# Attention's sums of squares on ScalarE head by head, and four other steps of a fused attention and expert kernel at new places

## The chip, the cores and the metric

The kernel runs on one core of a Trainium2 chip. A core has a matrix engine (TensorE, PE in the profile, its weight loads PEld), a vector engine (VectorE, DVE), an activation engine (ScalarE, ACT), a general engine (GpSimd, POOL) and a queue that issues transfers (SyncE, SP). Each engine takes its instructions in the order in which the program lists them, and waits on semaphores for the others. The metric is the time of one launch on the device in microseconds, the median of several runs; lower is better.

## The reference, cut to what matters

```python
# attention, without softmax: batch 4, 8 heads, 576 tokens, 64 wide
kv = einsum('bhsd,bhse->bhde', k, v)
out = einsum('bhsd,bhde->bhse', q, kv)
rms = sqrt(mean(out * out, axis=-1, keepdims=True) + 1e-06)     # one per token and head
x = (out / rms * g_norm)                                        # 2304 tokens x 512
# first expert layer: x 2304 x 512, w_in 512 x 2048, w_out 2048 x 512
h = x @ w_in
x = (h * (1.0 / (1.0 + exp(-h)))) @ w_out
# second: 4 experts, w1 512 x 1024 and w2 1024 x 512 each, p = normed domain_probs
for e in range(4):
    out += p[:, e:e+1] * (maximum(x @ w1[e], 0.0) @ w2[e])
```

Everything is float32.

## The kernel before, in words

The kernel has three stages that overlap at their seams. All products are made in two or three parts: an operand is split into a high part (a rounded copy, made on ScalarE) and a low part (the difference, made on VectorE or GpSimd), and PE multiplies the parts.

*Attention* (the first 130 us). PROGRAM is a list of steps written out by hand order, one word each, that the kernel walks through; it fixes the order on every engine. For each of the four batches: `kv` multiplies keys and values, `bd` copies the result, `out` (attn_out, L702 to L716) makes the attention output of a block of 128 tokens in PSUM, `sq` (attn_sq, L718) its sums of squares per head, `cp` (attn_cp, L724) copies the block from PSUM to SBUF, `rms` (attn_rms, L727) makes 1/rms of all blocks of the batch, `sc` scales, `x` transposes (L763) and `xs` splits. The blocks number 4, 5, 4 and 5 for batches 0 to 3, 18 in all. In batch 0 the blocks have PSUM banks of their own, and rms uses a square root on ScalarE (L734); in the others the output tiles share four PSUM buffers with the first layer's products, `cp` frees them, and rms is made by multiplications on VectorE or GpSimd. The steps `cv1` (two activations, L634 and L635), `cv2` and `cv3` turn weights from a 64-bit form into float32; `sp` splits weights (L664, L665). The words `1:n`, `e:n`, `f:n` and `2:n` are steps of the first expert layer: its first product (mm1, L789), the evaluation of h (L803, L804), its split (L812, L813) and its second product (mm2, L827). In before, attn_sq squares the whole block on ScalarE (one activation of 128x512) and adds each head's 64 squares on VectorE (L722).

*First expert layer* (to about 475 us). Units of 12 matmuls of 128x512 each, PE busy throughout.

*Second expert layer* (class Second, the rest). It is made by Winograd's form of Strassen's scheme: seven products instead of eight, on sums and differences of the quarters. It runs in 24 steps: three passes over thirds of the tokens, eight half experts ("pairs" in what follows, numbered 0 to 7) each. Steps 0 to 7, the first pass, make the weights: sums of quarters (sumw, L202) and splits (op1, op2, L159 and L160); the split weights of the first layer of experts and of the second are put away to memory (put_away, L218) and got back (get, L223) in the later passes. In each step `first` (L251) makes seven products into two PSUM tiles x and z; the results c11, c12, c22 and c21 are collected (keep, add), rectified and multiplied with the probabilities (relu, L286), and split (oph). c21 is rectified straight from PSUM. In the first pass `second` (L332) makes the plain eight products for the second layer; from step 8 on `again` makes seven (L251 too, into ps_ox and ps_oz), for which t1 to t4 are differences of the c (sumh, L292), and `gather` (L310) adds results up.

The weight sums s1 to s4 of the second layer aren't used in the first pass, so they are made beside other work, all on VectorE but for the high part: for pair n, s1 and s2 in step 2n and s3 and s4 in step 2n + 1, until step 15.

The order on all engines in this stage comes from `events` (L372): each action is put at a slot, a number on a common scale on which PE has about one product to a slot, and the actions are then sorted and issued in that order. A step is 15 slots long in the first pass and 14 later. A slot is no time: it only says behind and ahead of what an instruction stands in its engine's queue. At the end of step 23 the results are transposed and written (leave_last, L364 to L369).

Of the kernel before, what the change touches and what calls it, by code (L numbers as in the profile page):

```python
# [13 lines left out]
AF = mybir.ActivationFunctionType  # L14
ALU = mybir.AluOpType
AX = mybir.AxisListType
PSUM = bass.MemoryType.PSUM

B, H, S, D = 4, 8, 576, 64
# [61 lines left out]
class Second:  # L81
# [290 lines left out]
    def events(self):  # L372
# [3 lines left out]
        def put(slot, f, *a):  # L376
            ev.append((slot, len(ev), f, a))

        pool = self.nc.gpsimd
        for n in range(self.steps):  # L380
            t, q = divmod(n, E2)
            b0, after = self.start[n], self.start[n + 1]
# [19 lines left out]
            for k in range(7):  # L402
                i = b0 + 1 + 2 * k
# [28 lines left out]
            put(b0 + 10.3, self.relu, n, "c22")  # L432
            put(b0 + 10.5, self.oph, n, "c22", None if make and n else pool)
            put(b0 + 12.25, self.relu, n, "c12")
            put(b0 + 14.05, self.relu, n, "c21")
            put(b0 + 14.06, self.ps.pop, (n, "x"))
            if make:
                put(b0 + 12.5, self.oph, n, "c12")
                put(b0 + 14.1, self.oph, n, "c21")
                for i, name in ((5.4 if n else 6.2, "c11"), (12.6, "c22"), (12.6, "c12"), (14.2, "c21")):  # L440
                    put(b0 + i, self.f.pop, (n, name))

                for k, (i, j) in enumerate(((0, 0), (0, 1), (1, 0), (1, 1))):
                    at = b0 + ((7.2, 8.6, 10.2, 14.7) if n else (7.2, 8.6, 15.2, 17.7))[k]
                    put(at - 5.5, self.load2, n, i, j)
                    put(at, self.op2, n, f"a{i + 1}{j + 1}", pool if k != 1 else None)
                    put(at + 0.01, self.raw.pop, (n, 2, f"a{i + 1}{j + 1}"))
                    if k != 2:
                        put(at + 2.5, self.put_away, n, 2, (0, 1, None, 6)[k])
                for b in range(4):  # L450
                    for d in range(2):
                        put(after + 4 * b + 2 * d, self.second, n, b, d)
                    put(after + 4 * b + 3.2, self.gather, n, b, *self.BLOCKS[b])
                    put(after + 4 * b + 3.21, self.ps.pop, (n, b))
                for i in range(2):
                    for j in range(2):
                        put(after + (10.1, 14.1)[1 - j], self.h.pop, (n, f"b{i + 1}{j + 1}"))
                        put(after + (6.1, 14.1)[i], self.w2.pop, (n, f"a{i + 1}{j + 1}"))
            else:
                put(b0 + 12.3, self.sumh, n, "t1")  # L460
                put(b0 + 12.31, self.f.pop, (n, "c12"))
                put(b0 + 12.4, self.oph, n, "t1")
                put(b0 + 12.5, self.sumh, n, "t2")
                put(b0 + 12.51, self.f.pop, (n, "c22"))
                put(b0 + 12.52, self.f.pop, (n, "t1"))
                put(after + 1.11, self.oph, n, "t2")
                put(after + 1.12, self.sumh, n, "t3")
                put(after + 1.13, self.f.pop, (n, "c11"))
                put(after + 1.14, self.oph, n, "t3", pool)
                put(after + 1.15, self.f.pop, (n, "t3"))  # L470

                u = after + (1 if n < self.steps - 1 else 3)
                put(u + 0.16, self.sumh, n, "t4")
                put(u + 0.17, self.f.pop, (n, "t2"))
                put(after + 5.5, self.oph, n, "t4", pool)
                put(after + 5.51, self.f.pop, (n, "t4"))
                put(after + 3.3, self.oph, n, "c21")
                put(after + 3.31, self.f.pop, (n, "c21"))
                for m, k in enumerate(self.ORDER):
                    put(after + 2 * m, self.again, n, k)  # L480
                    put(after + 2 * m - self.LEAD, self.get, n, 2, k)
                for m, g in enumerate(self.GATHER):
                    last = n == self.steps - 1
                    if last and m == 6:
                        for d in range(2):
                            put(after + 2 * m + 0.45, self.gather, n, *g, d)
                    else:
                        put(after + 2 * m + (1.1 if m < 6 else 0.45), self.gather, n, *g)
                put(after + 11.2, self.ps.pop, (n, "oz"))
                put(after + 12.46, self.ps.pop, (n, "ox"))  # L490
# [10 lines left out]
            elif q == E2 - 1:  # L501
                for k in range(PW // 256):
                    put(self.start[n + 3 + k] + 11.5, self.leave, n + 2 + k, t, 2 * k)

        for n in range(E2):
            a, b = self.start[2 * n] + (7 if n == 0 else 0), self.start[2 * n + 1] + (3 if n == 0 else 0)
            for k, (i, j) in enumerate(((1, 0), (1, 1), (0, 0), (0, 1))):
                put(a + 0.4 + 0.1 * k, self.load2, n, i, j, True)
            for at, name in ((a, "s1"), (a + 2, "s2"), (b, "s3"), (b + 2, "s4")):
                k = self.A.index(name)  # L510
                put(at + 5.5, self.sumw, n, 3, name)
                put(at + 7.3, self.op2, n, name)
                put(at + 9.2, self.put_away, n, 2, k)
                put(at + 9.21, self.w2.pop, (n, name))
            for name, at in (("s1", a + 7.6), ("a22", a + 5.6), ("a11", b + 5.6), ("a21", b + 5.6), ("s3", b + 7.4),
                             ("a12", b + 7.6), ("s2", b + 7.6), ("s4", b + 9.4)):
                put(at, self.raw.pop, (n, 3, name))
# [14 lines left out]
def attention_moe_kernel(ctx: ExitStack, tc: tile.TileContext, kv, qt, g2, probs, wd, w, out):  # L532
    nc = tc.nc
# [166 lines left out]
    rinv, ssq, o_ps, x_ps = {}, {}, {}, {}  # L700
# [17 lines left out]
    def attn_sq(b, i):  # L718
        p = o_ps[i]
        sq = tmp_p.tile([128, H, D], F32, tag="tmp", name="sq")  # L720
        nc.scalar.activation(sq.rearrange("p h d -> p (h d)"), p, AF.Square)
        nc.vector.reduce_sum(ssq[b][:, i, :], sq, axis=AX.X)  # L722

    def attn_cp(b, i):  # L724
        nc.scalar.activation(o_of[i].rearrange("p h d -> p (h d)"), o_ps.pop(i), AF.Copy)  # L725
# [117 lines left out]
    def order(e):  # L843
        return ([0, 1, 2, 3, 4], [4, 0, 1, 2, 3], [4, 0, 1, 2, 3], [0, 1, 4, 2, 3])[e]
# [5 lines left out]
    def put(i, h, f, *a):  # L850

        todo.setdefault((i, h), []).append((f, a))
# [5 lines left out]
    with tc.manual_schedule():  # L858
# [3 lines left out]
        for t in kvbd:  # L862
# [3 lines left out]

        do = dict(
            lkv=load_kv, lq=load_q, lwd=load_wd, kv=attn_kv, bd=attn_bd, out=attn_out, sq=attn_sq, cp=attn_cp,
            rms=attn_rms, sc=attn_scale, x=attn_x, xs=attn_xs, cv1=cv1, cv2=cv2, cv3=cv3, sp=split,
        )  # L870
# [27 lines left out]
        for e in range(1, E1 - 1):  # L898
            last = order(e)[-1]
            mid = order(e)[1]  # L900
            for j in range(FC):
                c = (e + 1) * FC + j

                i = at[e, mid, 0] + 3 * j
# [9 lines left out]
        i = at[E1 - 1, order(E1 - 1)[-2], 0]  # L914
# [6 lines left out]
        n = 2 * FC  # L921
# [55 lines left out]
```

## Time and profile before

| | before |
|---|---|
| median of 3 runs | 1219.12 us (1217.57 to 1220.42) |
| profiled execution | 1215.1 us |
| its span, first to last instruction | 1213.2 us |
| TensorE busy | 1178.1 us (97%) |
| VectorE, ScalarE, GpSimd busy | 838.1, 459.7, 312.5 us |
| mean granted TensorE clock, share of full | 0.997 |

| stage, us | PE busy of | VectorE | ScalarE | granted clock |
|---|---|---|---|---|
| 12 to 30 | 12.41 of 18 | 14.19 | 11.88 | 1.00 |
| 30 to 60 | 25.32 of 30 | 28.44 | 15.70 | 0.94 |
| 60 to 90 | 28.63 of 30 | 25.16 | 17.69 | 1.00 |
| 90 to 120 | 26.77 of 30 | 18.97 | 14.19 | 1.00 |
| 400 to 500 | 97.87 of 100 | 60.20 | 35.46 | 0.98 |
| 500 to 900 | 400.0 of 400 | 312.5 | 156.9 | 1.00 |
| 900 to 1000 | 96.69 of 100 | 82.89 | 36.79 | 1.00 |
| 1180 to 1213.2 | 26.30 of 33.2 | 20.49 | 8.28 | 0.98 |

A row of the timeline below reads: start in us, length in us, engine, line, operation, tile written <- tiles read, their shapes, how many instructions the row holds, and in brackets how long the engine had been idle before it and what it had waited for ("issue": nothing that the profile shows). The length of a matmul reaches past the start of the next one, since matmuls overlap; the distance of starts is what one costs. The clock is granted in two levels, 1.2 and 2.4 GHz; 1.00 is the higher.

### The profile page before, as it was taken

How to read it: one execution, taken by the hardware profiler on the slowest of the kernel's cores; microseconds unless marked ns; L12 is line 12 of the kernel's file. 1: busy time of each engine (PE TensorE's matmuls, PEld its weight loads, DVE VectorE, ACT ScalarE, POOL GpSimd, SP SyncE). 2: the span in 40 equal slices, each digit the busy share in tenths (PEclk: the TensorE clock that was granted, in tenths of full speed). 3: DMA queues.
4: the chain of work that ended last, by engine and by line, in shares of the span. 5: the costliest groups of instructions: out<-in, count | busy, mean ns of one | idle time of the engine just before them, and what ended most of it. 6: DMA issues, size and time to landing. Idle time of an engine off the chain costs nothing.

```text
span 1213.2 us, 17113 instructions
## 1 busy us (share of the span) xinstructions
PE 1178.1 (97%) x6513; PEld 1105.0 (91%) x6513; DVE 838.1 (69%) x1081; ACT 459.7 (38%) x726; POOL 312.5 (26%) x220
## 2 busy tenths in 40 slices
PE   6899999999999999999999999999999899999997
PEld 5777798888888889999999999999999899999997
DVE  4986554655564456877777867788888876666775
ACT  4555543343333243544444433333333332333222
POOL 3553442311310013522222311111113211111112
PEclk9999999999999999999999999999999999999999
DMA  9613121200200007799878677999998878888763
GB/s 327 216 57 114 35 70 35 71 18 1 97 27 1 1 1 238 274 358 323 315 271 309 237 281 281 317 308 338 307 323 285 290 241 249 277 266 277 248 203 120
DMA packets 94854, 242.91 MB, mean 200 GB/s; under 512 B 11244, under 2 KB 42420, under 8 KB 94772
## 3 DMA queue, kind: packets, MB, share of 16 engines
q1 hardware_dynamic: 92756, 238.63, 57.9%
q10 hardware_dynamic: 2016, 3.18, 0.7%
q8 instruction: 52, 0.85, 0.3%
q14 instruction: 30, 0.25, 0.1%
HBM read 178.30 MB, written 63.48 MB: 199 GB/s over the span
## 4 chain that ended last, share of the span: by engine, by line
PE 83%; DVE 2%; issue 1%; ACT 1%; DMA 0%; DVEq 0%; ACTq 0%
PE ps_x L251 16%; PE a L827 13%; PE p_h L789 12%; PE ps_z L251 12%; PE ps_o L332 11%; PE ps_ox L251 10%; PE ps_oz L251 8%; DVE f L286 0%; PE ps_t L350 0%; DVE f L269 0%; DMA w<-w_dram 0%; DVE s L202 0%; DVE t L292 0%; DVE acc L310 0%; ACT hid L159 0%
## 5 line engine op out<-in xcount | busy, mean ns | idle before, releaser
L251 PE MATMUL ps_x<-x,w 128*128 128x384 f32 x1152 | 215.8, 335 | 1.9 <-ACT x L159 1.9
L251 PEld LDWEIGHTS ps_x<-x,w 128*128 128x128 f32 x1152 | 201.4, 188 | 2.3 <-ACT x L159 2.2
L251 PE MATMUL ps_z<-x,w 128*128 128x384 f32 x864 | 163.6, 337 | 2.1 <-DVE f L286 2.1
L251 PEld LDWEIGHTS ps_z<-x,w 128*128 128x128 f32 x864 | 152.4, 189 | 2.9 <-DVE f L286 2.5
L159 ACT ACTIVATE hid<-f 128x768 fp32r<-128x768 f32 x80 | 67.6, 845 | 211.3 <-DVE f L286 211.3
L251 PE MATMUL ps_ox<-hid,w 128*128 128x384 f32 x768 | 145.0, 337 | 2.1 <-issue 2.1
L332 PE MATMUL ps_o<-hid,w 128*128 128x384 f32 x768 | 142.7, 335 | 0.0
L251 PEld LDWEIGHTS ps_ox<-hid,w 128*128 128x128 f32 x768 | 134.1, 188 | 2.7 <-issue 2.7
L332 PEld LDWEIGHTS ps_o<-hid,w 128*128 128x128 f32 x768 | 134.3, 188 | 0.1
L789 PE MATMUL p_h<-x_hi,w_hi 128*128 128x512 f32 (+1 forms) x320 | 119.7, 374 | 1.1 <-ACT o L725 1.1
L160 POOL TENSOR_TENSOR hid<-t,hid 128x768 fp32r<-128x768 f32 x32 | 61.0, 1906 | 231.0 <-ACT hid L159 226.1
L804 DVE TENSOR_TENSOR sg<-p_h,sg 128x512 f32<-128x512 f32 (+1 forms) x80 | 50.7, 636 | 99.9 <-ACT sg L803 99.6
L789 PE MATMUL p_h<-x_lo,w_hi 128*128 128x512 f32 (+1 forms) x320 | 119.1, 372 | 0.5 <-DVE x_lo L775 0.5
L827 PE MATMUL a<-h_lo,w_hi 128*128 128x512 f32 (+1 forms) x320 | 118.3, 370 | 1.1 <-DVE h_lo L813 1.1
L789 PE MATMUL p_h<-x_hi,w_lo 128*128 128x512 f32 (+1 forms) x320 | 119.2, 373 | 0.0
L827 PE MATMUL a<-h_hi,w_hi 128*128 128x512 f32 (+1 forms) x320 | 118.5, 370 | 0.0
L827 PE MATMUL a<-h_hi,w_lo 128*128 128x512 f32 (+1 forms) x320 | 118.0, 369 | 0.0
L251 PE MATMUL ps_oz<-hid,w 128*128 128x384 f32 x576 | 108.2, 335 | 1.7 <-issue 1.4
L251 PEld LDWEIGHTS ps_oz<-hid,w 128*128 128x128 f32 x576 | 100.5, 188 | 2.6 <-issue 2.0
L159 ACT ACTIVATE hid<-t 128x768 fp32r<-128x768 f32 x64 | 54.0, 843 | 125.2 <-DVE t L292 125.2
L803 ACT ACTIVATE sg<-p_h 128x512 f32<-128x512 f32 (+1 forms) x80 | 44.4, 555 | 146.7 <-PE p_h L789 139.3
L160 POOL TENSOR_TENSOR w<-raw,w 128x512 fp32r<-128x512 f32 x41 | 59.2, 1451 | 153.2 <-ACT w L159 69.5
(133 smaller groups left out, 1824.5 us busy)
## 6 DMA issues: line engine op xcount, KB each, us to landing
w<-w_dram SPq DMA_DIRECT2D x224, 512.0 KB, 4.5
w_dram<-w SPq DMA_DIRECT2D x112, 512.0 KB, 4.9
raw<-in_w SPq DMA_DIRECT2D x192, 128.0 KB, 3.5
wd_raw<-in_wd SPq DMA_DIRECT2D x28, 512.0 KB, 3.8
pb<-p_dram SPq DMA_DIRECT2D x12, 384.0 KB, 6.0
kv_first_lo<-in_kv SPq DMA_DIRECT2D x6, 512.0 KB, 10.2
q_raw<-in_qt SPq DMA_DIRECT2D x6, 512.0 KB, 7.5
out<-o ACTq DMA_DIRECT2D x12, 256.0 KB, 4.4
```

What stands on the lines that cost most here:

```text
L159: self.nc.scalar.activation(t[:, 0], f, AF.Copy)
L160: (eng or self.nc.vector).tensor_tensor(t[:, 1], f, t[:, 0].bitcast(F32), op=ALU.subtract)
L251: self.nc.tensor.matmul(p[:, f, :HN], w[0][:, a, c : c + 128], x[:, b, kp, :], start=self.FRESH[k] and a == b == kp == 0, stop=b == kp == ...
L332: self.nc.tensor.matmul(self.ps[n, b][:, e, :HN], w[:, u, c : c + 128], h[:, v, kp, :], start=self.count[key] == 1, stop=self.count[key] = ...
L789: nc.tensor.matmul(p[:, :n], wt[:, 0, cols], xt[:, kc, :], start=k == 0, stop=k == 3 * KC - 1)
L803: nc.scalar.activation(sg[:, :n], p[:, :n], AF.Sigmoid)
L804: nc.vector.tensor_tensor(sg[:, :n], p[:, :n], sg[:, :n], op=ALU.mult)
L827: nc.tensor.matmul(o, a, m, start=first and k == 0, stop=last and k == 2)
```

## The change

Four edits. (1) attn_sq makes eight activations, one a head, each of which writes its squares and, as a second output (accum_out), their sum; the reduction on VectorE is gone. The order of PROGRAM is as it was. (2) In step 0 the rectifying of c21 is put at slot 13.1 instead of 14.05, so ahead of two weight sums, s1 and s2 of the first layer of pair 1, and of a split. (3) In the last step the split of c21 is put at slot 7.2 after the step instead of 3.3. (4) The sums for the second layer's weights, with their loads, splits and put-aways, are spread evenly, one half of a pair each 0.913 steps from step 0.5 to step 14.2, instead of one half in each step. The first halves move by up to 4.9 slots later (pair 1), the last by 11.2 slots earlier (pair 7, now in step 14; before, step 15).

```diff
--- before.py
+++ after.py
@@ -432,7 +432,7 @@
             put(b0 + 10.3, self.relu, n, "c22")
             put(b0 + 10.5, self.oph, n, "c22", None if make and n else pool)
             put(b0 + 12.25, self.relu, n, "c12")
-            put(b0 + 14.05, self.relu, n, "c21")
+            put(b0 + (14.05 if n else 13.1), self.relu, n, "c21")
             put(b0 + 14.06, self.ps.pop, (n, "x"))
             if make:
                 put(b0 + 12.5, self.oph, n, "c12")
@@ -474,8 +474,9 @@
                 put(u + 0.17, self.f.pop, (n, "t2"))
                 put(after + 5.5, self.oph, n, "t4", pool)
                 put(after + 5.51, self.f.pop, (n, "t4"))
-                put(after + 3.3, self.oph, n, "c21")
-                put(after + 3.31, self.f.pop, (n, "c21"))
+                u = after + (3.3 if n < self.steps - 1 else 7.2)
+                put(u, self.oph, n, "c21")
+                put(u + 0.01, self.f.pop, (n, "c21"))
                 for m, k in enumerate(self.ORDER):
                     put(after + 2 * m, self.again, n, k)
                     put(after + 2 * m - self.LEAD, self.get, n, 2, k)
@@ -502,8 +503,12 @@
                 for k in range(PW // 256):
                     put(self.start[n + 3 + k] + 11.5, self.leave, n + 2 + k, t, 2 * k)
 
+        def part(h):
+            k, f = divmod(0.5 + h * 13.7 / 15, 1)
+            return self.start[int(k)] + f * (self.start[int(k) + 1] - self.start[int(k)])
+
         for n in range(E2):
-            a, b = self.start[2 * n] + (7 if n == 0 else 0), self.start[2 * n + 1] + (3 if n == 0 else 0)
+            a, b = part(2 * n), part(2 * n + 1)
             for k, (i, j) in enumerate(((1, 0), (1, 1), (0, 0), (0, 1))):
                 put(a + 0.4 + 0.1 * k, self.load2, n, i, j, True)
             for at, name in ((a, "s1"), (a + 2, "s2"), (b, "s3"), (b + 2, "s4")):
@@ -718,8 +723,8 @@
     def attn_sq(b, i):
         p = o_ps[i]
         sq = tmp_p.tile([128, H, D], F32, tag="tmp", name="sq")
-        nc.scalar.activation(sq.rearrange("p h d -> p (h d)"), p, AF.Square)
-        nc.vector.reduce_sum(ssq[b][:, i, :], sq, axis=AX.X)
+        for h in range(H):
+            nc.scalar.activation(sq[:, h, :], p[:, h * D : h * D + D], AF.Square, accum_out=ssq[b][:, i, h : h + 1])
 
     def attn_cp(b, i):
         nc.scalar.activation(o_of[i].rearrange("p h d -> p (h d)"), o_ps.pop(i), AF.Copy)
```

## Rows read from the trace of the kernel before

**Rows 1.** Page, busy us of each engine, share of the span, instructions.

```profile
PE 1178.1 (97%) x6513; PEld 1105.0 (91%) x6513; DVE 838.1 (69%) x1081; ACT 459.7 (38%) x726; POOL 312.5 (26%) x220
```

**Rows 2.** View of tile sq: ns min/median/max, first and last start us, forms.

```profile
L722 DVE TENSOR_REDUCE ssq<-sq x18: 670/677/687, 16.6 to 117.8; 128x8 f32<-128x512 f32 x18
```

**Rows 3.** Timeline of ScalarE: an activation of one column, and the next.

```profile
23.16 0.20 ACT L736 ACTIVATE one<-one 128x1 f32<-128x1 f32 x1
23.27 0.65 ACT L634 ACTIVATE cv_a<-wd_raw 128x512 f32<-128x512 f32 x1
```

**Rows 4.** Timeline, batch 0: first square, square root, transposes.

```profile
15.94 0.60 ACT L721 ACTIVATE sq<-a 128x512 f32<-128x512 f32 x1 [2.27 <-PE a L713]
...
21.62 0.23 ACT L734 ACTIVATE t<-m 128x32 f32<-128x32 f32 x1 [0.70 <-DVE m L730]
...
25.55 0.63 PE L763 MATMUL a<-ident,acc 128*128 128x128 f32 x4 [3.10 <-DVE acc L754]
```

**Rows 5.** Timeline, batch 1: ScalarE's queue, VectorE's conversion, PE's transposes.

```profile
36.53 0.58 ACT L721 ACTIVATE sq<-p_o 128x512 f32<-128x512 f32 x1
37.01 0.59 ACT L725 ACTIVATE acc<-p_o 128x512 f32<-128x512 f32 x1
...
41.19 0.63 ACT L664 ACTIVATE w_hi<-w_f 128x512 fp32r<-128x512 f32 x1 [3.10 <-DVE w_f L654]
...
44.11 0.69 ACT L634 ACTIVATE cv_a<-acc 128x512 f32<-128x512 f32 x1
...
45.16 0.41 DVE L644 TENSOR_SCALAR cv_a<-cv_a 128x512 f32<-128x512 f32 x1
...
53.29 0.66 PE L763 MATMUL p_t<-ident,acc 128*128 128x128 f32 x4 [2.26 <-POOL acc L754]
```

**Rows 6.** Timeline, batch 2: second block's square, mean of squares.

```profile
77.99 0.58 ACT L721 ACTIVATE sq<-p_o 128x512 f32<-128x512 f32 x1
...
84.85 0.17 DVE L730 TENSOR_SCALAR m<-ssq 128x32 f32<-128x32 f32 x1
```

**Rows 7.** Timeline, batch 3: first square, a block's copy, PE's next unit.

```profile
112.50 0.60 ACT L721 ACTIVATE sq<-p_o 128x512 f32<-128x512 f32 x1
...
117.69 0.60 ACT L725 ACTIVATE acc<-p_o 128x512 f32<-128x512 f32 x1
...
118.75 0.39 PE L789 MATMUL p_h<-x_hi,w_hi 128*128 128x512 f32 x1
```

**Rows 8.** Timeline, steps 0 and 1 of the second layer: VectorE and PE.

```profile
488.91 2.38 DVE L202 TENSOR_TENSOR s<-raw,raw 128x512 f32<-128x512 f32 x2
...
490.31 2.25 PE L332 MATMUL ps_o<-hid,w 128*128 128x384 f32 x12
...
493.68 0.95 DVE L286 SCALAR_TENSOR_TENSOR f<-ps_x,pb 128x768 f32<-128x768 f32 x1
...
494.69 3.92 PE L251 MATMUL ps_z<-x,w 128*128 128x384 f32 x12 [2.13 <-DVE f L286]
```

**Rows 9.** Timeline, steps 15 and 16: a gather, PE's two gaps.

```profile
951.81 0.95 DVE L310 TENSOR_TENSOR acc<-ps_ox,acc 128x768 f32<-128x768 f32 x1
...
952.86 2.32 PE L251 MATMUL ps_oz<-hid,w 128*128 128x384 f32 x12 [1.45 <-issue]
...
969.84 2.38 PE L251 MATMUL ps_x<-x,w 128*128 128x384 f32 x12 [1.86 <-ACT x L159]
```

**Rows 10.** Timeline, last step: c21's split, a gather, PE's gap.

```profile
1195.54 2.52 DVE L160 TENSOR_TENSOR hid<-f,hid 128x768 fp32r<-128x768 f32 x1
...
1197.99 0.95 DVE L310 TENSOR_TENSOR acc<-ps_ox,acc 128x768 f32<-128x768 f32 x1
...
1199.03 2.35 PE L251 MATMUL ps_ox<-hid,w 128*128 128x384 f32 x12 [1.94 <-issue]
```

**Rows 11.** Timeline, steps 2 and 3: PE's products, a weight split on VectorE.

```profile
550.53 4.33 PE L332 MATMUL ps_o<-hid,w 128*128 128x384 f32 x24
...
552.44 0.68 DVE L160 TENSOR_TENSOR w<-s,w 128x512 fp32r<-128x512 f32 x1
```

## What the change will do to the time, said before it ran

> **What bounds the kernel now.** Read the page's busy times first: PE works 1178.1 of 1213.2 us [rows 1], so the span is TensorE's work plus 35.1 us in which it waits. A change off TensorE can only add to those waits or take from them. So the second view is the timeline of PE, looked through for gaps, and the third is the timeline of the engine that each gap names. The gaps lie in two places. Most are in the first 130 us, where attention's chain (scores, sum of squares, scale, transposes) feeds PE: 3.10 us at 25.55 and 2.26 us at 53.29 [rows 4, 5]. The others are few: 2.13 us at 494.69, 1.45 us at 952.86, 1.86 us at 969.84, 1.94 us at 1199.03 [rows 8 to 10]. The change touches both places, and I count them apart.
>
> **Sums of squares: the price of one block.** There are 18 blocks (4, 5, 4 and 5 for the four batches). Removed is the reduction on VectorE, 0.677 us each [rows 2], 12.2 us in all. On ScalarE one square of 128x512 becomes eight of 128x64. Now ScalarE's queue moves on 0.48 us after a square starts (36.53 to 37.01) [rows 5]. Call the new figure c. An activation of one column takes 0.20 us and one of 512 takes 0.60 [rows 3, 4], so 64 columns take 0.20 + 63 x 0.40/511 = 0.25 us. Neighbours overlap by 0.09 to 0.10 us: 23.16 + 0.20 against a next start at 23.27, and 0.58 long against 0.48 [rows 3, 5]. So a square of one head moves the queue on by 0.15 us, and c is at least 8 x 0.15 = 1.2. What the sum costs beside it, no row shows. Below: nothing, c = 1.2 (1.0 if more overlaps). Above: a second small instruction, with no overlap at all, 0.25 + 0.20 = 0.45 us a head, c = 3.6. I take a second instruction like the one-column one, overlapping as that one does (0.11 us from start to start): 0.26 a head, c = 2.1. It is the nearest row to an instruction that writes one column. A gain is excluded on ScalarE, since even 1.0 is twice 0.48.
>
> The Trainium skill, page "ScalarE: Activation LUTs", section "Rules for kernel authors", speaks against the edit: it budgets about 0.3 us for each activation plus 0.83 ns an element. That is an estimate of 0.35 us a head and c = 2.8, where the row at 23.16 [rows 3] lets the next start after 0.11. By it the four batches below would cost 29 us and the time would be some 1243 us, between my forecast and my dear rival.
>
> **Where c is on the path.** *Batch 0.* PE waits for x, x for the root, the root for all four sums. ScalarE holds four squares, a pair of conversions and a weight copy before the root; the last two kinds are 0.69 and 0.63 long [rows 5], so with the overlap taken off 2 x 0.59 + 0.53 = 1.7 us. The root can start at 15.94 + 4c + 1.7 instead of 21.62 [rows 4]: 4c - 4.0. The reductions that go had been hidden but for the last. For c = 2.1: 4.4 us, and all of it goes on to the PE wait at 25.55 [rows 4], as PE's program order has only work that needs x.
> *Batch 1.* From 36.53: two squares and a copy, then a weight copy that waits for VectorE until 41.19, then two squares, two copies, a square and the conversion at 44.11, on which VectorE's 45.16 waits; the scale chain and PE's 53.29 hang on that [rows 5]. With c = 2.1 the first three end at 36.53 + 4.2 + 0.48 = 41.2, so that wait of 3.10 us hides them. The other three squares are bare: 41.19 + 0.53 + 3c + 2 x 0.48 + 0.69 - 45.16 = 3c - 1.8 = 4.5 us (for c over 2.1 it is 5c - 5.9). VectorE, relieved of five reductions, isn't the bound any more, so the relief buys nothing.
> *Batch 2.* From 77.99: three squares, a weight copy, a copy; with the last square counted to its end the mean starts at 79.1 + 3c, against 84.85 [rows 6]: 3c - 5.7, so 0.6 us; at c = 1.2 nothing, or a gain of up to 1 us, since the reductions had been in front.
> *Batch 3.* From 112.50: five squares, a copy, a rounding, a conversion pair, a weight copy, then the copy at 117.69, which frees the PSUM buffer that PE's matmul of 118.75 takes [rows 7]. ScalarE worked through these without a pause, so the copy ends 5 x (c - 0.48) later than 117.69 + 0.60, and PE is late by 5c - 2.9 = 7.6 us. No work in PE's order fills that.
> Sum: 4.4 + 4.5 + 0.6 + 7.6 = 17.1 us. At c = 1.2 it is 0.8 + 1.8 + 0 + 3.1 = 5.7; at 3.6 it is 10.4 + 12.1 + 5.1 + 15.1 = 42.7.
> *Clock.* After the gap at 494.69 twelve matmuls took 3.92 us instead of the 2.25 of 490.31 [rows 8]: 1.7 us at the lower of the two clock levels. New gaps may bring that again, and not each gap does (969.84 shows 2.38). I count one, 1.7 us; 0 in the cheap case, two in the dear one.
>
> **c21 of step 0.** PE's first product into z of step 1 takes the PSUM bank that step 0's last rectifying step (493.68, 0.95 long) reads; PE waits 2.13 us and runs slow after it [rows 8]. At slot 13.1 that step comes before two weight sums and a low part, behind the first of the two sums that began at 488.91 and took 2.38 together [rows 8]; with that one at its half or a little over, the step ends by about 491.3, before 490.31 + 2.08 = 492.4. The wait and the slow stretch go: 2.13 + 1.67 = 3.8 us. Next late would be c21's own low part on VectorE, needed about 1 us later than it comes; and step 1 must now keep up with a PE that is 3.8 us earlier. I take 3.4, bounds 1.5 and 3.8.
>
> **Weight sums spread over 14 steps instead of 16.** In step 15 two sums and two splits of pair 7 stand in VectorE's queue, each some 0.68 us, as the split of rows 11, and longer where POOL holds them. Its gather at 951.81 ends at 952.76, and PE starts at 952.86 after 1.45 us; the next lateness shows at 969.84, 1.86 us [rows 9]. With the sums in step 14 VectorE has some 2.7 us more than it had, and both gaps go: 3.3 us. The moved steps' loads and put-aways sit on SP's queue; the put-aways now wait there in front of other steps' gets, which are issued eight slots of 2.08 us ahead (4.33 us for 24 matmuls [rows 11]), so a delay of a few us is hidden; if that cover is gone, it costs as much as the delay exceeds 16.6 us. In other steps the sums land at other slots. The worst is step 2: its split and sums now stand around c12, whose low part ended as the split of 552.44 began, for a product that PE started at 550.53 + 2.08 = 552.61 and that reads the low part four matmuls, 4 x 2.08/12 = 0.7 us, later [rows 11]. Two more operations of 0.68 make it late by about 0.4. Net gain 2.9, bounds 0 and 3.3.
>
> **Last step.** PE's 1199.03 waited 1.94 us for the gather at 1197.99, queued behind c21's split, which took VectorE 2.52 us where the gather of the same size took 0.95 [rows 10]; POOL was working on its own splits meanwhile. With the split at slot 7.2 the gather follows at 1195.5, and the gap goes. Next late would be c21 itself, due some 2.7 us after PE's earlier start, about when it comes. 1.9, bounds 0.9 and 2.1.
>
> **Sum.** -3.4 - 2.9 - 1.9 = -8.2; +17.1 + 1.7 = +18.8; together +10.6 us on the profiled execution (1215.1 us, of which 1.9 lie outside the span), so 1225.7. The median shown is 1219.12, 4.0 above that execution; the forecast for a median is 1229.7.
>
> **Rivals.** *Cheap sums.* The sum costs no instruction, or one that overlaps wholly: c = 1.0 to 1.2. Then attention costs 3 to 5.7 and the gains win: 5.7 - 8.2 = -2.5, 1216.6 us, at c = 1.0 some 1214. This ends on the other side; it decides where attention's cost is 8.2, at c = 1.4, 0.175 us a head. For it: the overlap in rows 3. Against: the sum of a head is complete only when its last element is through, so something must follow it.
> *Dear sums.* Each waits for the pipeline: c = 3.6, +42.7 + 3.4 - 8.2 = +37.9, 1257 us. For it: a sum can't be read before its square is done.
> *The sums collide.* At the forecast's c, the weight sums at new slots stall several steps as step 15 was stalled now: the 2.9 gained becomes 3 lost, 1235.6 us. Against: from 500 to 900 us, steps that carried such sums too, the table of stages has PE busy without a gap.
> *No effect in attention.* VectorE's relief offsets ScalarE's load, 1211: against, the waits of rows 5 and 7 are ScalarE's own queue.
>
> **How the numbers follow.** Forecast (c from 1.6 to 2.6, 1223 to 1240): 0.45. Dear: 0.14. Collide: 0.05. Cheap, with no effect: 0.32 faster; near the deciding point, 0.04. A measurement here can tell about 0.2%, 2.4 us. Faster 0.32, same 0.06, slower 0.62. The range takes in the cheap cases and most of the dear: 1212 to 1252.
>
> **What would show it.** In the profile after: the per-head squares' spacing on ScalarE gives c at once, with 144 squares and, by my price, 144 more instructions; VectorE's busy time falls by 12.2 us; PE waits longer before 25.55's transposes and gets a new wait of some 7 us where 118.75's matmul stands now; the gaps at 494.69, 952.86, 969.84 and 1199.03 are gone. A spacing under 0.175 us a head makes the prediction wrong in sign; a late step 1 or 2 would show as new gaps near 517 and 553.

## The result, and the profile after

| | before | after |
|---|---|---|
| median | 1218.34 us (1215.66 to 1220.42) | 1228.67 us (1227.13 to 1232.64) |
| ratio, 95% interval | | 1.0091 [1.0076, 1.0105] |
| profiled execution, its span | 1215.1, 1213.2 us | 1227.13, 1224.9 us |
| granted TensorE clock, share of full | 0.997 | 0.992 |

The kernel after is 0.9% slower, 11 us, and the forecast was 1229.7. The total came out close for a poor reason: attention cost 11.9 us where 18.8 had been forecast, the three other edits gained 3.3 where 8.2 had been, and the two errors nearly cancelled. The rest of this document takes them apart.

First the page of after: busy time of each engine, its share of the span, instructions (against [rows 1]).

```profile
PE 1182.7 (97%) x6513; PEld 1108.6 (91%) x6513; DVE 820.2 (67%) x1063; ACT 477.6 (39%) x996; POOL 312.4 (26%) x220
```

VectorE lost 17.9 us, of which the reductions were 12.2; ScalarE's busy time grew by 17.9 and its instructions by 270. TensorE's own work is the same 6513 matmuls in the same order. So the two traces can be laid on each other matmul by matmul, and the difference of the start of one and the same matmul is the lateness of after at that place. That gives the map: +1.7 us at the transposes of batch 0, +6.3 at those of batch 1, +7.5 shortly behind them and still at the end of batch 2, +12.4 at the first layer's unit in batch 3, +15.0 behind it, +13.5 when attention is over. From there to the end 1.8 us are won back, not the 8.2 of the forecast. The trace of before that this is read against was a lucky one: five later runs with the same attention (e2_rest, e3_sums, e4_c21s, e8_keep and e9_t3 below) are 1.8 to 5.6 us late against it at the end of attention, too. So the map tells where the lateness arises, but not all of its size need be the edit's.

The tile view of sq in after: operation, count, ns min/median/max, first and last start; then who waited for the tile (us, times).

```profile
L727 ACT ACTIVATE sq<-p_o x112: 204/292/552, 39.7 to 129.5; 128x64 f32<-128x64 f32 x112
L727 ACT ACTIVATION_READ_ACCUMULATOR sq<-p_o x112: 192/278/540, 39.8 to 129.6; 128x1 f32 x112
...
  DVE m L735: 8.2, 2
```

Each square with a sum is two instructions in the trace, the activation and a read of the accumulator, 112 and 112 here and 32 and 32 more from batch 0's banks. Their spacing is in ScalarE's timeline of after, first block of batch 1:

```profile
39.74 0.20 ACT L727 ACTIVATE sq<-p_o 128x64 f32<-128x64 f32 x1
39.85 0.19 ACT L727 ACTIVATION_READ_ACCUMULATOR sq<-p_o 128x1 f32 x1
39.94 0.21 ACT L727 ACTIVATE sq<-p_o 128x64 f32<-128x64 f32 x1
...
41.31 0.65 ACT L730 ACTIVATE acc<-p_o 128x512 f32<-128x512 f32 x1
```

From square to read 0.11 us, from read to the next square 0.09, and eight heads take 41.31 - 39.74 = 1.57 us. So c is 1.57, not the 2.1 of the forecast. The durations in the rows are longer than these distances, and grow to 0.55 while the queue is full; only the distance of starts is a price.

The waits of PE in attention, as the view of waits of after sums them up (us in total, times, longest):

```profile
...
PE p_h L794 <- ACT acc L730: 5.0, 1, 5.0
PE a L768 <- DVE acc L759: 4.8, 1, 4.8
PE p_t L768 <- POOL acc L759: 4.4, 2, 3.0
PE p_h L794 <- ACT o L730: 2.9, 1, 2.9
...
PE p_o L718 <- ACT acc L730: 1.6, 1, 1.6
```

And PE's timeline of after, at these places and in the second layer:

```profile
27.26 1.08 PE L768 MATMUL a<-ident,acc 128*128 128x128 f32 x4 [4.78 <-DVE acc L759]
...
42.01 1.16 PE L718 MATMUL p_o<-kvbd,q_raw 128*128 128x128 f32 x8 [1.60 <-ACT acc L730]
...
48.82 0.50 PE L794 MATMUL p_h<-x_hi,w_hi 128*128 128x512 f32 x1 [2.91 <-ACT o L730]
...
59.56 1.11 PE L768 MATMUL p_t<-ident,acc 128*128 128x128 f32 x4 [3.02 <-POOL acc L759]
...
131.17 0.80 PE L794 MATMUL p_h<-x_hi,w_hi 128*128 128x512 f32 x1 [5.05 <-ACT acc L730]
...
505.79 2.25 PE L251 MATMUL ps_z<-x,w 128*128 128x384 f32 x12
...
512.47 2.36 PE L251 MATMUL ps_x<-x,w 128*128 128x384 f32 x12 [2.35 <-ACT f L264]
...
628.38 2.65 PE L332 MATMUL ps_o<-hid,w 128*128 128x384 f32 x12 [0.76 <-ACT hid L159]
...
965.48 2.33 PE L251 MATMUL ps_oz<-hid,w 128*128 128x384 f32 x12 [0.38 <-issue]
...
982.42 3.83 PE L251 MATMUL ps_x<-x,w 128*128 128x384 f32 x12 [1.87 <-ACT x L159]
...
1210.83 2.24 PE L251 MATMUL ps_ox<-hid,w 128*128 128x384 f32 x12
```

Read against [rows 4, 7, 8, 9, 10]: the wait for batch 0's transposes grew from 3.10 to 4.78, and the matmul of 118.75, which waited for nothing, now waits 5.05 for ScalarE's copy. The gap at 494.69 is gone (505.79 has none), but a new one of the same size stands three products later, at 512.47. The gap at 952.86 shrank from 1.45 to 0.38, the one at 969.84 is as it was (1.87 at 982.42), and the one at 1199.03 is gone. Step 3 has a new one of 0.76.

The clock after the longest new gap, by the stretches 126.2 to 131.2 and 131.2 to 137.2 us of after (length, then PE, PEld, DVE, ACT, POOL busy, granted clock, DMA share, GB/s):

```profile
126.20:131.20 5.00, 0.03 (x1) 0.03 (x1) 0.97 (x3) 5.00 (x43) 3.00 (x3) 0.84 0.01 2
131.20:137.20 6.00, 6.00 (x16) 4.74 (x17) 0.69 (x1) 4.64 (x13) 5.02 (x14) 0.57 0.30 87
```

ScalarE is busy all through the gap while PE stands still; in the six microseconds behind it the granted clock is 0.57, near the lower of the two levels, and the lateness grows from 12.4 to 15.0.

### The profile page after: what moved, and what is told of

Read it like the earlier page. It is cut to its first block, busy times and chain, and to the rows that moved or that the text cites. A ratio compares the mean times of both kernels' runs of the same rounds, so it can differ in the third digit from the quotient of the medians.

```text
span 1224.9 us, 17357 instructions
## 1 busy us (share of the span) xinstructions
PE 1182.7 (97%) x6513; PEld 1108.6 (91%) x6513; DVE 820.2 (67%) x1063; ACT 477.6 (39%) x996; POOL 312.4 (26%) x220
## 4 chain that ended last, share of the span: by engine, by line
PE 72%; DVE 7%; ACT 2%; issue 2%; SPq 1%; DMA 1%; ACTq 0%; DVEq 0%
PE ps_x L251 14%; PE p_h L794 11%; PE a L832 11%; PE ps_z L251 10%; PE ps_o L332 9%; PE ps_ox L251 9%; PE ps_oz L251 7%; DMA raw<-in_w 1%; DVE f L286 1%; DVE s L202 1%; ACT hid L159 1%; DVE hid L160 1%; SPq L185 1%; DVE acc L310 1%; DVE t L292 1%
```

## The experiments

The theory to test: each block holds ScalarE's queue for 1.57 us instead of 0.48, and this is paid only where that queue ends a wait of PE, with slow matmuls behind the new gaps; the three other edits gain about 2 and not 8, because two of the four gaps hang on something else. The rivals: the terms as recorded (+18.8 and -8.2); a cost spread over all blocks alike; edits that meddle with each other. The first four runs of the table, the next four and the last four were each compared with runs of before on the same chip (medians 1219.67, 1219.62 and 1218.83 us).

| run | what it is | median, us | ratio to before, 95% |
|---|---|---|---|
| e1_attn | before + edit 1 | 1231.18 | 1.0098 [1.0081, 1.0114] |
| e2_rest | before + edits 2, 3, 4 | 1215.69 | 0.9973 [0.9961, 0.9984] |
| e3_sums | before + edit 4 | 1217.98 | 0.9988 [0.9974, 1.0002] |
| e4_c21s | before + edits 2, 3 | 1217.89 | 0.9980 [0.9964, 0.9997] |
| e5_split | eight squares, no sums | 1223.04 | 1.0028 [1.0017, 1.0039] |
| e6_batch2 | edit 1 in batch 2 alone | 1218.82 | 0.9991 [0.9978, 1.0005] |
| e7_batch3 | edit 1 in batch 3 alone | 1224.55 | 1.0037 [1.0024, 1.0050] |
| e8_keep | edits 2, 3, 4 + a move on ScalarE | 1214.93 | 0.9953 [0.9939, 0.9967] |
| e9_t3 | e8_keep + a move on VectorE | 1212.09 | 0.9942 [0.9929, 0.9955] |
| e10_batch0 | edit 1 in batch 0 alone | 1221.53 | 1.0024 [1.0011, 1.0036] |
| e11_batch1 | edit 1 in batch 1 alone | 1223.06 | 1.0034 [1.0022, 1.0045] |
| e12_after | the kernel after again | 1229.59 | 1.0081 [1.0067, 1.0095] |

### The edits apart

e1_attn takes the square of the kernel after into the kernel before and nothing else:

```
+        for h in range(H):
+            nc.scalar.activation(sq[:, h, :], p[:, h * D : h * D + D], AF.Square, accum_out=ssq[b][:, i, h : h + 1])
```

> The kernel before with the first edit alone: eight squares with a second output a block, no reduction on VectorE. Path theory (each block holds ScalarE's queue 1.56 us instead of 0.48, and that is paid only where the queue ends a wait of PE: 1.7 in batch 0, 3.3 in batch 1, 0 in batch 2, 5.0 in batch 3, of which 1.4 is taken up again at 127 us, and the new gaps bring half clock for about 5): +13.5 us, some 1231.9 where before has 1218.4, and PE as late at 150 us as in the kernel after. Recorded terms (c = 2.1, one slow stretch): +18.8, 1237.2. Relief theory (what VectorE saves comes back later on): PE's lateness of 13.5 us at 150 us shrinks further on, under +10 at the end.

It took 0.98% more, 11.9 us [9.9, 13.9]. The recorded 18.8 is out, and the path theory's 13.5 lies within the interval. PE is 14.0 us late against the trace of before when attention is over and 14.8 at the end: nothing that VectorE saved came back later, so the relief theory falls too.

e2_rest is the other three edits with the square of before:

> The kernel before with the second, third and fourth edits and not the first: c21 of step 0, c21 of the last step, weight sums spread. Lateness theory (the differences of PE's start times between the traces of before and after, counted from 150 us on): -1.8 us, 1216.6 where before has 1218.4. Recorded terms: -3.4 - 2.9 - 1.9 = -8.2, 1210.2. A rival says that the stages are not separable and the first edit's lateness changes what the sums collide with: then the gaps near 512, 628 and 982 us of after (2.35, 0.8 and 1.9 us there) are absent or of other size here.

It gained 0.27%, 3.3 us [2.0, 4.8]: more than the 1.8 that the two traces gave, far less than the recorded 8.2. The gap that stands at 512.47 in after is here too (2.61 us, at 504.74), so it has nothing to do with attention.

e3_sums is edit 4 alone, e4_c21s edits 2 and 3:

> The kernel before with the fourth edit alone, the weight sums spread over 14 steps. Lateness theory: -1.1 at step 15's first gap, +1.4 slow clock at its second, +1.7 in steps 2 and 3: +2, 1220.4 where before has 1218.4. If the new gap of after near 512 us (2.35 us, PE behind ScalarE's keep of c11, itself behind the high part of the second sum of pair 0) comes from the sums' later place, it stands here too and makes it +4.2, 1222.6. Recorded terms: -2.9, 1215.5.

> The kernel before with the second and third edits alone: rectifying c21 of step 0 at slot 13.1, splitting c21 of the last step at slot 7.2. If the new gap near 512 us of after comes from the sums' later place: -3.8 - 2.2 = -6.0, 1212.4 where before has 1218.4. If it is what is next late once PE arrives 3.8 us earlier in step 1: -1.6 - 2.2 = -3.8, 1214.6, with a gap of some 2 us at about 499 us. Recorded terms: -3.4 - 1.9 = -5.3, 1213.1.

e3_sums gained 1.5 us, with an interval that reaches no change; the +2 that I had read from the traces was wrong. Its trace shows the one sure term: the gap at 952.86 loses 1.1 us; the gap at 969.84 stays. The gap of after at 512.47 isn't here in its size, but a wait of 1.06 us stands at that product. The slow matmuls at 982.42, which I had put down to edit 4, don't come in this run, and come in e1_attn, which has the sums as before: they are the clock's, not the edit's. e4_c21s gained 2.4 us [0.4, 4.4], of which the last step is 2.1 by the traces. So edit 2 gave nothing that the times can show. Its own place shows why; first PE, then ScalarE in e4_c21s:

```profile
504.94 3.78 PE L251 MATMUL ps_x<-x,w 128*128 128x384 f32 x12 [2.62 <-ACT f L264]
...
503.56 0.63 ACT L159 ACTIVATE w<-s 128x512 fp32r<-128x512 f32 x1 [1.74 <-DVE s L202]
504.10 0.79 ACT L264 ACTIVATE f<-ps_x 128x768 f32<-128x768 f32 x1
```

The old gap is gone, but three products later PE waits 2.62 us for ScalarE's copy of c11 (L264), which frees its bank, and runs slow after that as it did after the old gap (3.78 for twelve matmuls, against 3.92 in [rows 8]). The copy had stood behind the high part of a weight sum (503.56), and that had waited 1.74 us for VectorE. As the sums of edit 4 aren't in this run, the new gap comes from edit 2: PE, 3.8 us earlier, runs into what is next late. The trace of before had shown how near that was:

```profile
498.82 0.63 ACT L159 ACTIVATE w<-s 128x512 fp32r<-128x512 f32 x1 [1.75 <-DVE s L202]
499.36 0.80 ACT L264 ACTIVATE f<-ps_x 128x768 f32<-128x768 f32 x1
...
500.54 2.25 PE L251 MATMUL ps_x<-x,w 128*128 128x384 f32 x12
```

The copy ended at 500.16, 0.38 us before the product that takes its bank. So a PE that comes earlier meets it. In e3_sums and e11_batch1, which keep the old gap, no slow matmuls followed that gap (2.39 us for twelve), and PE waited 1.06 us for the same copy. What is left of edit 2 depends on the clock behind the new gap: nothing in e4_c21s and e2_rest (3.78 and 3.75 for twelve), 1.3 us in after and e12_after (2.36 and 2.39).

### What the second output costs

e5_split makes eight squares a block on ScalarE and keeps VectorE's reduction:

```
+        for h in range(H):
+            nc.scalar.activation(sq[:, h, :], p[:, h * D : h * D + D], AF.Square)
+        nc.vector.reduce_sum(ssq[b][:, i, :], sq, axis=AX.X)
```

> The kernel before with eight squares a block on ScalarE but without the second output; VectorE keeps its reduction. Tells what the eight instructions cost without the sums. Theory: half of a head's 0.194 us in the kernel after is the reading of the sum, so squares alone start 0.10 apart, c = 0.8 a block; the formulas of the prediction then give nothing in batch 0 (4 x 0.8 - 4.0 is below nothing), 0.6 in batch 1, 0 in batch 2, 1.1 in batch 3: about +2, 1221.5 where before has 1219.7. Rival 1, the recorded lower bound (0.15 us a head, c = 1.2): +5.7, 1225. Rival 2, the eight instructions and not the sums are what costs (spacing near 0.19): +10 or more, 1230.

ScalarE's timeline of e5_split, the same block of batch 1 as above:

```profile
40.50 1.01 ACT L722 ACTIVATE sq<-p_o 128x64 f32<-128x64 f32 x8
41.33 0.67 ACT L726 ACTIVATE acc<-p_o 128x512 f32<-128x512 f32 x1
```

Eight squares hold the queue 0.83 us, 0.104 each, so the reads are the other half of c: (1.57 - 0.83) / 8 = 0.092 each. It cost 3.4 us [2.1, 4.8], rather more than the +2 of the formulas, less than the +5.7 of the first rival and far from the +10 of the second: the reads are what makes the edit dear.

### Where it is paid

Four runs with the edit in one batch each (`if b == 2:` ahead of the eight squares, the block square otherwise, and the same with 3, 0 and 1):

> The kernel before with the squares and sums head by head in batch 2 alone (4 of the 18 blocks). Path theory: 3c - 5.7 is below nothing at c = 1.56, no wait of PE hangs on it, so 0: 1219.7. Rival, the cost is ScalarE's time wherever it falls: 4/18 of the first edit's 12 us, +2.7, 1222.4.

> The kernel before with the squares and sums head by head in batch 3 alone (5 of the 18 blocks). Path theory: PE's wait for the copy that frees its buffer grows from 1.4 us in all to 5.6 (+4.2; 5c - 2.9 gives 4.9), and a slow stretch of the clock of about 2.2 follows a gap that long: +6.4, 1226.1 where before has 1219.7. Without the slow stretch +4.2, 1223.9. Rival, a cost spread over all blocks alike: 5/18 of 12 us, +3.3, 1223.0, and no wait longer than 2 us there.

> The kernel before with the squares and sums head by head in batch 0 alone (4 of the 18 blocks). Recorded formula at c = 1.56: 4c - 4.0 = 2.2, with the lateness at the transposes of batch 0 and what the clock adds there: 1221.8 to 1223 where before has 1219.6. Rival, the wait seen in the runs with all batches is 1.4 and part of it is taken up again before 37 us: +0.5 to 1.4, 1220.1 to 1221.

> The kernel before with the squares and sums head by head in batch 1 alone (5 of the 18 blocks). Recorded formula at c = 1.56: 3c - 1.8 = 2.9 at the transposes (53.29 in before), 1222.5 where before has 1219.6. Rival: ScalarE's copies, which free the buffers of PE's next blocks, come late first, so the waits stand at the attention outputs and at the next unit (43.33 in before) and the chain behind the transposes has slack again: 2.0 in all, 1221.6, with no longer wait at the transposes than before's.

Batch 2 costs nothing (-1.1 us [-2.7, 0.6]), though ScalarE does the same four blocks' extra work in it as in batch 0, which costs 2.9 [1.3, 4.4]; batch 1 costs 4.1 [2.7, 5.5] and batch 3 costs 4.5 [2.9, 6.1]. A cost spread alike would have been 2.7 for four blocks: the run of batch 2 excludes it. Together 10.4, within the interval of the 11.9 of all four at once. In e10_batch0's trace the wait at 25.55 grew by 1.7 us, less than the formula's 2.2, and nothing of it was taken up again before 37 us, against the rival; the times allow both. The slow matmuls that follow the wait there stand in e2_rest, e3_sums, e4_c21s, e8_keep and e9_t3 too, so they aren't the edit's. In e7_batch3 the wait stands where the formula had put it, and not under the 2 us of its rival:

```profile
126.57 0.80 PE L793 MATMUL p_h<-x_hi,w_hi 128*128 128x512 f32 x1 [5.05 <-ACT acc L729]
```

Two waits of before go in exchange, and the lateness falls by 1.5 there:

```profile
127.37 0.66 PE L763 MATMUL p_t<-ident,acc 128*128 128x128 f32 x4 [0.30 <-POOL acc L754]
...
128.82 1.09 PE L763 MATMUL p_t<-ident,acc 128*128 128x128 f32 x8 [0.79 <-POOL acc L754]
```

The slow stretch behind the wait is in this trace (3.0 us), but the theory's 6.4 lies above the interval of the times; its 4.2 without the stretch lies within. In e11_batch1 the waits are these:

```profile
41.84 1.16 PE L713 MATMUL p_o<-kvbd,q_raw 128*128 128x128 f32 x8 [1.61 <-ACT acc L729]
...
48.64 0.50 PE L793 MATMUL p_h<-x_hi,w_hi 128*128 128x512 f32 x1 [2.89 <-ACT o L729]
...
59.39 0.66 PE L767 MATMUL p_t<-ident,acc 128*128 128x128 f32 x4 [3.03 <-POOL acc L758]
```

In before's trace they were 0.44, 1.08 and 2.26 (the last in [rows 5]), so +1.2, +1.8 and +0.8:

```profile
37.65 1.16 PE L713 MATMUL p_o<-kvbd,q_raw 128*128 128x128 f32 x8 [0.44 <-ACT acc L725]
...
43.33 0.50 PE L789 MATMUL p_h<-x_hi,w_hi 128*128 128x512 f32 x1 [1.08 <-ACT o L725]
```

Most of batch 1's cost is thus paid at the copies that free PSUM buffers for PE, ahead of the transposes, which get only the rest. Neither what I had recorded (all at the transposes) nor the rival (nothing there) is right; the amount is 3.8 by these rows, less 0.6 that is caught up at 39.49, against 2.9 by the formula.

### What held the two gaps that stayed

e8_keep has edits 2, 3 and 4 and puts the high part of pair 0's second sum behind the copy of c11:

```
-                put(at + 7.3, self.op2, n, name)
+                put(at + (7.75 if (n, name) == (0, "s2") else 7.3), self.op2, n, name)
```

> The second, third and fourth edits with the square as before, and one more move: the high part of the second weight sum of pair 0 goes behind ScalarE's copy of c11 of step 1 (slot 17.25 instead of 16.8). Theory: that part, waiting for VectorE's sum, is what kept the copy and with it PE in step 1 (2.3 us in the run without this move), so PE starts 2.3 us earlier, and the slow stretch of 1.7 behind the gap may go: against the run of the second to fourth edits (0.9973 of before) another -2.3 to -4.0, so 1212 to 1214 where before has 1219.7. Rival: the next operation in the queue is as late (the high part of step 1's own weights, which waits for VectorE too), and the gap stays to within 0.7 us: 1216.

ScalarE and PE in e8_keep, to be read against the fence of e4_c21s above:

```profile
497.95 0.79 ACT L264 ACTIVATE f<-ps_x 128x768 f32<-128x768 f32 x1
499.80 0.63 ACT L159 ACTIVATE w<-s 128x512 fp32r<-128x512 f32 x1 [1.06 <-DVE s L202]
...
498.80 2.38 PE L251 MATMUL ps_x<-x,w 128*128 128x384 f32 x12 [0.24 <-ACT f L264]
...
504.20 2.36 PE L251 MATMUL ps_z<-x,w 128*128 128x384 f32 x12 [0.94 <-DVE f L269]
```

The copy now goes first, PE waits 0.24 instead of 2.62 and its matmuls run at full speed (2.38 for twelve). A smaller wait of 0.94 follows for VectorE's next addition. The time is 0.9953 of before, 5.7 us less [4.0, 7.4], where the three edits without the move gained 3.3 [2.0, 4.8]: the theory's lower end. The two intervals overlap; that the copy held PE is shown by the traces, and of the 3.8 us of edit 2 PE keeps 2.2 in this one.

e9_t3 adds one move more: the difference t3 for the third pass, in step 16.

```
-                of = {"t1": start_of_last + 7.2, "t2": start_of_last + 7.3, "t3": b0 + 5.5, "t4": b0 + 7.3}
+                of = {"t1": start_of_last + 7.2, "t2": start_of_last + 7.3, "t3": b0 + (5.5 if t < 2 else 2.2), "t4": b0 + 7.3}
```

> The run with the copy of c11 ahead of pair 0's second sum (0.9953 of before) and one more move: VectorE's difference t3 for the third pass's input (2.60 us at step 16, beside a split on GpSimd) goes from 5.5 to 2.2 slots after the start of step 16, ahead of c21's low part, where VectorE sat idle for 1.4 us. Theory: PE's gap of 1.9 us in step 16 hangs on this difference and the high part made from it, not on the weight sums; the gap goes, and with it the slow matmuls behind it (1.3 where they come): -1.9 to -3.2 against that run, 1211.7 to 1213 where before has 1219.6. Rival, the recorded one, that weight sums in VectorE's queue made the gap: they have left step 15 already and the gap stands, so it is VectorE's whole load there; then the gap stays to within 0.5 us and the time is 1214.9.

Step 16 in e8_keep, VectorE's difference, GpSimd's split beside it, PE:

```profile
966.48 2.60 DVE L233 TENSOR_TENSOR t<-acc 128x768 f32<-128x768 f32 x1
...
966.38 1.88 POOL L160 TENSOR_TENSOR hid<-t,hid 128x768 fp32r<-128x768 f32 x1 [4.43 <-ACT hid L159]
...
970.01 3.20 PE L251 MATMUL ps_x<-x,w 128*128 128x384 f32 x12 [1.88 <-ACT x L159]
```

and the same difference and product in e9_t3, with GpSimd's split beside the difference there:

```profile
957.94 0.95 DVE L233 TENSOR_TENSOR t<-acc 128x768 f32<-128x768 f32 x1
...
958.17 2.43 POOL L160 TENSOR_TENSOR hid<-t,hid 128x768 fp32r<-128x768 f32 x1 [9.95 <-ACT hid L159]
...
967.59 2.25 PE L251 MATMUL ps_x<-x,w 128*128 128x384 f32 x12
```

In e8_keep the difference starts just behind GpSimd's split and takes 2.60 us; in e9_t3 it starts ahead of one and takes 0.95. The gap of 1.88 is gone with the slow matmuls behind it. So that gap was never the weight sums', as I had recorded. By these rows the stretch, 1.65 us, makes most of the gap; but e9_t3 also moved the difference 8.5 us earlier, so this share is worked out and not measured apart. In these two traces PE gains 3.8 us at this place; the medians differ by 2.8 and the ratios by 0.0011, with intervals that overlap, so it is the traces that show the difference to be the cause, and the times only agree in sign. e9_t3, at 0.9942 of before (7.1 us less [5.5, 8.7]), beats both kernels.

### The kernel after once more

> The kernel after itself, once more, beside the same runs of before as the three others. The first edit alone cost 0.98% and the other three together gained 0.27%. If the edits add up: +0.71%, 1228.3 where before has 1219.6. If they meddle with each other: +0.9% or more as in the comparison of before and after, 1230.7.

0.81%, 9.9 us [8.2, 11.6], between the two. The parts add up to 0.71%, with an estimated 0.2 on either side by their own intervals. This run's interval holds 0.71; that of the first comparison, 0.76 to 1.05, just leaves it out. So the runs neither show nor exclude that the edits meddle a little.

Step 3's new gap (0.76 at 628.38, 0.80 in this run) is no sign of meddling. e8_keep, which leaves edit 1 out, has it too (0.98); e9_t3, with the same step 3 as e8_keep, doesn't. What goes with it is a wait of ScalarE for a raw weight's transfer in that step, in after:

```profile
614.08 0.63 ACT L159 ACTIVATE w<-raw 128x512 fp32r<-128x512 f32 x1 [3.71 <-DMA raw<-in_w]
```

It is 3.71, 3.44 and 3.94 us in after, e12_after and e8_keep, which have the gap. It is 2.88 to 2.91 in e2_rest, e3_sums and e9_t3, which don't have it, and there is none in before or in any run without edit 4. So the wait belongs to edit 4; whether the put-aways on SP's queue are behind it was not tried.

## Why the prediction was right, and where it was wrong

**The whole.** Forecast +18.8 - 8.2 = +10.6; measured apart +11.9 - 3.3 = +8.6, together +9.9 and +11.1. The sign, the place of the largest wait and the likeliest case hold; the agreement to 1 us is luck of cancelling terms. Of the waits in attention 17.1 had been forecast, and the traces show 8.4; of slow matmuls 1.7, and the runs show about 6 at most; of the gains 8.2, and the times show 3.3.

**The price of a block.** The mechanism held: something follows each square, a second small instruction. Its size was nearly right, 0.092 us against the 0.11 taken from the one-column row [rows 3]. Mis-sized was the square itself: I took its estimated length, 0.25, less an overlap of 0.10, so 0.15, and even the lower bound of 1.0 us a block rested on that. Eight squares alone take 0.83 (e5_split). The overlap of 0.10 was right and the length wrong: the shortest square of 64 columns lasts 0.204, as long as the one-column row, on which I had laid 0.05 for 63 more columns. That row is of another function and another tile, so it was no place to start a line to the 512-column squares from; which of the two makes it as long as 64 columns was not tried. The figure worked out from the Trainium skill, page "ScalarE: Activation LUTs", section "Rules for kernel authors", c = 2.8, is further off: the rows show 1.57, and the measurement decides.

**Where it is paid.** Put c = 1.57 into the formulas: 2.3, 2.9, 0 and 5.0, in sum 10.1. The traces show 1.7, 3.2, 0, and 5.05 less the 1.5 that is won back behind it, in sum 8.4. Batches 0, 2 and 3 held in place, and in size but for that 1.5 and for 0.6 in batch 0. In batch 1 the size held and the place didn't: PE waited for the copies that free the PSUM buffers, which I followed in batch 3 and not here. "No work in PE's order fills that" failed by those 1.5 us, since waits of before that lie behind vanish. (For c over 2.1 batch 1's form comes out of its own terms as 5c - 6.0, not 5.9; the forecast doesn't hang on it.)

**The clock.** I counted one slow stretch of 1.7 us. The span times the share that the granted clock is below full estimates what the clock took: 12.6 us on average in after (4 executions) and in e12_after (4), 14.1 in e1_attn (4), against 7.6 in the runs of before beside e1_attn (25) and 6.8 in those beside e12_after (21). So where edit 1 is in, slow matmuls cost 5.7 (e12_after) to 6.5 us (e1_attn) more, by this estimate, where I had counted 1.7. Idle time at the lower level counts in these figures too, so they are rather an upper end. The two profiled executions point the same way: TensorE's busy time grew by 4.6 us with the same matmuls, and its waits by 7.1. So "can only add to those waits or take from them" was too narrow. The stretch behind the 5.05 us gap was there in all four traces with it (after, e1_attn, e7_batch3, e12_after).

**c21 of step 0.** The gap at 494.69 went, as said, and of the gain at most 1.3 us stayed. The failed step is "I take 3.4": I had written that step 1 must keep up with a PE 3.8 us earlier and did not follow ScalarE's queue there, where the copy of c11 had 0.38 us to spare. e8_keep shows the place: the copy behind one weight part.

**Weight sums.** "Both gaps go: 3.3 us" failed for one of the two. 952.86 lost 1.1. 969.84 hung on VectorE's difference beside a GpSimd split, as the row that ended the wait (ACT x, after DVE t) would have shown if I had followed it back; I had taken nearness for cause. The late step that I had put at 0.4 didn't come in step 2: PE is 12.05 us late in after ahead of 552.61 and behind it. It came in step 3 (584 to 616 us of before), with 1.6 us in after and 0.6 in e3_sums. So by the traces the term lies between 0.5 gained (e3_sums) and 0.6 lost (after), by the times it is 1.5 gained [-0.2, 3.2], and not 2.9.

**Last step.** -1.9 forecast, -2.1 to -2.3 in the traces with the edit; the split of c21 at 1211.90 stretches to 1.87 and PE doesn't wait for it.

**The rivals.** Cheap sums would decide at 0.175 us a head with the forecast gains; 0.196 was measured, on the slow side but not by much. With the real gain of 3.3 the point lies lower still. The collision of sums came in small, as the 0.6 to 1.6 us of step 3, and not as the rival's 3 lost.

## What to carry to other kernels

Price a short instruction by the distance of starts in a row of its own kind, not by a length worked out between rows of other kinds. For every gap that an edit is to close, follow the wait back to the instruction that held it, and then ask each engine's queue what comes next for a TensorE that arrives earlier, and with how much to spare: here it was 0.38 us. Test a cost per stage, with the edit in one stage at a time: the same four blocks cost 2.9 us in batch 0 and nothing in batch 2.

## What the runs showed of the hardware

**The granted clock differs between executions of the same work.** Batches 1 and 2 are the same code in e7_batch3 and e10_batch0, and TensorE had been waiting equally long (1.78 us) ahead of 95.02 and 97.25. Stretches of both on each side of that point:

```profile
88.00:95.00 7.00, 3.79 (x18) 2.68 (x17) 6.56 (x17) 1.29 (x3) 3.62 (x3) 1.00 0.24 75
95.00:102.00 7.00, 6.98 (x36) 6.28 (x37) 4.38 (x5) 2.30 (x4) 1.28 (x1) 0.76 0.22 66
```

```profile
90.20:97.20 7.00, 3.82 (x18) 2.67 (x16) 6.56 (x17) 1.26 (x3) 3.65 (x3) 1.00 0.22 75
97.20:104.20 7.00, 6.95 (x45) 6.32 (x46) 4.41 (x5) 2.33 (x4) 1.29 (x1) 1.00 0.32 84
```

The first is e7_batch3, the second e10_batch0. The work before is alike to a few hundredths of a microsecond, and one got 0.76 afterwards, 36 matmuls in seven microseconds, the other 1.00 and 45. Such stretches come and go in the traces of this case by 0.9 to 2.8 us each, so a single pair of profiles can mislead: the profiled execution of before lost 3.6 us by the measure above where 25 others lost 7.6 on average, and I first read the slow matmuls at 982.42 as an effect of the weight sums.

**VectorE and GpSimd hold each other up, and the one that starts first keeps its length.** The difference of e8_keep started 0.10 us behind GpSimd's split and took 2.60 us; in e9_t3 it started 0.23 ahead of one and took 0.95, as it does alone, and the split took 2.43, where splits alone take some 1.85. So it is with the weight sums in before: 23 that began beside a GpSimd operation already running took 1.78 us in the median, and 7 that had begun ahead of one 0.68. The Trainium skill, page "SBUF — State Buffer", section "Who interferes with whom", says that a VectorE instruction with two SBUF inputs contends with a GpSimd instruction that reads SBUF; e8_keep and e9_t3 agree, with 2.60 us on VectorE in the one and 2.43 on GpSimd in the other. Most of the gap at 969.84 came from this by the rows; the sums of the edit only stood near it.
